# Single row maxima as two 256-key halves on both sides of a score pair, ordered by a SyncE no-op

## The chip, the cores and the metric

The kernel runs on 1 core of a Trainium2 chip. The metric is the time in device microseconds of one execution. Five engines work side by side and wait for each other by semaphores: TensorE (PE for matmuls, PEld for the loading of their weights), VectorE (DVE), ScalarE (ACT), GpSimd (POOL) and SyncE (SP), which issues most DMAs here.

## The reference

For 2048 tokens of width 512 the kernel computes two attentions with 32 heads of 16 and mixes them by a gate. Branch A is a dilated local attention over 8 positions. Branch B is full attention with one key head and one value head that all 32 query heads share. The change lies in branch B:

```python
q = (x @ wq).reshape(B, S, H, Dh).transpose(0, 2, 1, 3)
k = x @ wk
v = x @ wv
scores = einsum("bhqd,bkd->bhqk", q, k) * (Dh ** -0.5)
p = softmax(scores, axis=-1)
...
return g * a + (1 - g) * b
```

The softmax needs the maximum of each query's 2048 scores before the exponentials, since the weights of B are large.

## The kernel before, in words

Branch B is cut into 32 units (4 blocks of 512 queries, 8 groups of 4 heads). A unit has 16 steps, one for each 128 keys, so there are 512 main steps.

In step `s`, `exp_pair` (L459) forms the scores of 128 keys for 512 queries of two heads. Head `odd = 0` uses rows 0 to 63 of the array and head `odd = 1` uses rows 64 to 127, so the two matmuls run beside each other. They write a tile of two banks (`pe` in the profile), and one ScalarE exponential of 1024 columns turns it into `pexp`. A step has two such pairs, on the tiles `eb[0]` and `eb[1]`. Then `weighted` (L473) multiplies the exponentials of step `s - 1` by the values, into `po`.

The maxima of a later unit are found between these. One maximum item is 128 queries against 512 keys of one head. `fill_pair` (L339) takes two heads at once: two matmuls on the two halves of the array into the two banks of `m2` (`pm`), and one VectorE reduction. `fill_one` (L350) takes one item: one matmul on one half of the array into the single bank `m1` (`ps`), and one reduction. A third way, `fill_diff` and `fill_sum`, takes two items with the help of ScalarE; it is used in the front of the program and in the three output phases, not in main steps. A unit needs 64 items (L39 counts them in all), and its maxima enter the query tile through small DMAs that SyncE issues (`shift_d`, L449) after two GpSimd operations (L441, L442).

The order of the work is written out by the program itself while it is built. It keeps its own clocks (`clk`, `free`) with assumed durations (L45) and asks at each place whether a bank is free by then. In the main loop (from L1218) a step is: first score pair, a pair of maxima if `m2` is free, a single maximum if `m1` is free and `singles` (L841) says that one is owed, second score pair, then `weighted`. `out_phase` (L762) projects a finished block; when it comes is decided by `LEAD` (L42), the lead of the maxima in units.

Each engine executes its own list in order. A wait that stands in TensorE's list holds all that is behind it.

Of the kernel before, what the change touches and what calls it, by code (L numbers as in the profile page):

```python
# [6 lines left out]
F32 = mybir.dt.float32  # L7
F32R = mybir.dt.float32r
AF = mybir.ActivationFunctionType
# [4 lines left out]
P = 128  # L14
# [34 lines left out]
def gated_mix_kernel(ctx, tc, xt, wa, wk, wq, wo_a, wo_b, out):  # L49
# [227 lines left out]
    def place(v):  # L277
        return v if v <= NB else (v - NB - 1) % (NB - 2)
# [18 lines left out]
    half = []  # L297
    free = {"m1": 0.0, "e0": 0.0, "e1": 0.0, "po": 0.0, "d0": 24.0, "d1": 24.0}
    tasks, shifted = [], set()
    hooks, pool, done = [], 0.0, set()  # L300
# [4 lines left out]
        marks.append((ups[0] if up is None else up, end, inst.ins.name))  # L305

    def fillable():
        return bool(half) or bool(slots) and slots[0][0] < len(stacked) and stacked[slots[0][0]] <= clk["pe"]

    def unit_tile(v):  # L310
        if v not in mx:
            mx[v] = wp.tile([P, 2, 2, 4, 4], F32, name="mx", bufs=3)
            if v < 2:
                nc.scalar.activation(mx[v].rearrange("p b i t k -> p (b i t k)"), ident[:, 0:64], AF.Identity, scale=0.0, bias=mk[:, 6:7])
            else:
                nc.gpsimd.memset(mx[v], -FMAX)
            left[v] = NF // NU
        return mx[v]
# [3 lines left out]
        nc.tensor.matmul(dst, qst[place(v)][b:b + 62, pr, t * P:(t + 1) * P], kst[b:b + 62, kc * 512:(kc + 1) * 512], start=True, stop=True)  # L322

    def to_go():
        return 2 * len(slots) + len(half)
# [23 lines left out]
    def fill_one(dst=m1, key="m1"):  # L349
# [8 lines left out]
        mark(got, free[key])  # L358
        filled(v, 1)


    kd, formed, ended = [], set(), set()
    pend, todo, read_d = [[], []], [[], []], [[0.0, 0.0], [0.0, 0.0]]
# [91 lines left out]
            shifted.add(v)  # L455


    pe, pexp, exped = [], {}, {}

    def exp_pair(s, pr):  # L460
        bank, key = eb[pr], f"e{pr}"
        u, kt = divmod(s, NJ)
        for odd in range(2):
            b = 64 * odd
            nc.tensor.matmul(bank[:, odd, :], kst[b:b + 64, kt * P:(kt + 1) * P], qst[place(u)][b:b + 64, pr, :], start=True, stop=True)  # L465
        e = px.tile([P, 2, 512], F32, name="pexp", bufs=6)
        got = nc.scalar.activation(e, bank, AF.Exp, scale=SCALE)  # L467
# [368 lines left out]

    tail, first = last_rows(), [0]

    owing = [0.0]

    def singles(s):  # L841

        steps = 16 * (NU - 1) - 8 - s
        if steps <= 0 or to_go() <= 0:
            return to_go() > 0
        owing[0] += (to_go() - 1.94 * steps - 15.5 * (NJ - 4 - outs)) / steps
        owing[0] = min(owing[0], 3.0)
        if s % 16 == 0 or owing[0] < 1.0 or clk["dve"] - clk["pe"] > 1.5 and owing[0] < 2.0:
            return False
        return True  # L850

    def fill_ready(key, slack):
        if fillable() and free[key] <= clk["pe"] + slack:
            clk["pe"] = max(clk["pe"], free[key])
            if key == "m1":
                fill_one()
            elif half and (not slots or half[0][0] < slots[0][0] or slots[0][0] >= len(stacked)):
                fill_one(m2[:, 0, :], "m2")
            elif slots:
                fill_pair(m2, "m2")  # L860
            return True

    def pause(most):
        n = 0
        while n < most and slots and fillable():
            key = min(("e0", "e1", "m2"), key=lambda k: free[k])
            clk["pe"] = max(clk["pe"], free[key])
            if half:
# [355 lines left out]
    for s in range(NS + 1):  # L1224
        u, kt = divmod(s, NJ)
        if len(stacked) < NU and s >= 16 * (gone(len(stacked)) + 1):
            stack(len(stacked))
        if s < NS and kt == 0 and u not in shifted:
            while u not in shifted:
                clk["pe"] += 0.5  # L1230
                run_tasks()
                if u not in shifted and left.get(u, 1):
                    assert pause(4)
        v = min(x[0][0] for x in (half, slots, [(NU,)]) if x)
        need = left.get(v, NF // NU)
        steps = 16 * v - 6 - s
        short = need - 2.8 * max(0, steps) if v < NU else 0
        lead = (NF - to_go()) / 64 - s / 16
        order = (0, "m2", "m1", 1) if s > 1 else (1, "m2", "m1", 0) if s else ()
        k, n = outs // 4, C - (outs >= NJ - 4)  # L1240
        if outs == NJ - 4:
            if short > 0 and steps < 2:
                pause(short)
        elif due or outs < NJ and outs // NH in done and kt == 15 and NHG * (k + 1) - 1 in shaped and (lead < LEAD or s >= 16 * (NHG * (k + 2) + 1) - 1):
            if not due:
                prepare(outs, n)
                due.append(n)
            else:
                out_phase(list(range(outs, outs + 4)), due.pop(), s)
                outs += 4  # L1250
        elif short > 0 and steps < 2:
            pause(short)

        for which in order:
            if which == "m2":
                if slots or half:
# [12 lines left out]
        run_tasks()  # L1269
        run_pool()  # L1270
    assert not slots and not half and not hooks and not tasks and first[0] > 12, (len(slots), len(hooks), len(tasks), outs)


    banks = [m2[:, 0, :], eb[0][:, 0, :], eb[1][:, 0, :], m1]
# [74 lines left out]
```

## Time and profile before

| | |
|---|---|
| median of 3 runs | 1475.54 us (1474.95 to 1475.56) |
| the profiled execution | 1475.06 us, of which the span of the instructions is 1473.1 us |
| TensorE matmul busy | 1459.5 us (99%) |
| ScalarE busy | 1303.7 us (89%) |
| VectorE busy | 1141.7 us (77%) |
| GpSimd busy | 951.0 us (65%) |

The main steps run from about 285 us to 1449 us of the span, with an output phase of some 34 us at 854, 1154 and 1287 us. A row of the timeline gives the start, the duration, the engine, the line, the operation, the tiles written and read, the count of instructions merged into it, and in brackets the idle time before it with what ended it.

### The profile page before, as it was taken

To read this page: it belongs to the slowest core of one execution; us is meant where nothing else is said; L and a number is where in the kernel's file an instruction comes from. 1 tells how busy PE (TensorE), PEld (TensorE's weight loads), DVE (VectorE), ACT (ScalarE), POOL (GpSimd) and SP (SyncE) were. 2 spreads that over 40 slices of the span, in tenths; PEclk is the share of its full clock that TensorE was granted. 3 is DMA by queue.
4 is the path that set the end of the run, shared out by engine and by line. 5 is a ranking of instruction groups with operands and counts; after the bars stand their busy time and mean duration, and the time that the engine had idled before them with its cause. 6 is when DMAs were issued, how large, how long until landed. Compare 5 with 4: busy or idle time off the path is not lost.

```text
span 1473.1 us, 29510 instructions
## 1 busy us (share of the span) xinstructions
PE 1459.5 (99%) x10965; PEld 742.9 (50%) x10965; DVE 1141.7 (77%) x1837; ACT 1303.7 (89%) x1706; POOL 951.0 (65%) x1693
## 2 busy tenths in 40 slices
PE   9999999999999999999999999999999999999998
PEld 6899999733333333333333383333333743383334
DVE  6778878788888888788888878888888678778821
ACT  5888988799999999999999989999999889889994
POOL 5731997888988988888888898898851311150000
PEclk9999999999999999999999999999999999999999
DMA  6653342320211210101202111121100000000000
GB/s 227 167 168 122 97 147 64 117 71 26 71 41 49 78 49 31 67 23 67 78 13 71 42 63 48 42 71 41 42 12 12 27 16 2 1 31 1 1 2 29
DMA packets 43911, 85.66 MB, mean 58 GB/s; under 512 B 9520, under 2 KB 25960, under 8 KB 39672
## 3 DMA queue, kind: packets, MB, share of 16 engines
q1 hardware_dynamic: 36632, 44.79, 10.1%
q0 software_dynamic: 6560, 37.95, 7.8%
q8 instruction: 86, 1.41, 0.4%
q10 hardware_dynamic: 576, 1.05, 0.2%
q14 instruction: 57, 0.47, 0.1%
HBM read 57.97 MB, written 25.25 MB: 56 GB/s over the span
## 4 chain that ended last, share of the span: by engine, by line
PE 94%; ACT 2%; POOL 1%; DVE 1%; DMA 0%; issue 0%; SPq 0%; POOLq 0%; ACTq 0%
PE po L476 34%; PE pe L465 25%; PE pf L1078 10%; PE pm L322 8%; PE ps L322 5%; PE pe L776 5%; PE pd L393 3%; ACT pexp L467 1%; PE po L322 1%; PE pf L193 1%; PE pe L1279 1%; DVE mx L344 0%; DMA ad<-stage 0%; PE pm L832 0%; PE ps L1279 0%
## 5 line engine op out<-in xcount | busy, mean ns | idle before, releaser
L467 ACT ACTIVATE pexp<-pe 128x1024 f32<-128x1024 f32 x1024 | 987.6, 1023 | 70.8 <-PE pe L465 68.1
L344 DVE TENSOR_REDUCE mx<-pm 128x2 f32<-128x1024 f32 x475 | 580.2, 1221 | 176.7 <-PE pm L322 174.6
L476 PE MATMUL po<-pexp,vst 128*32 128x512 f32 x4096 | 545.5, 605 | 0.1
L465 PE MATMUL pe<-qst,kst 64*128 64x512 f32 x1984 | 518.2, 459 | 4.7 <-ACT pexp L467 2.7
L465 PEld LDWEIGHTS pe<-qst,kst 64*128 64x128 f32 x1984 | 207.8, 183 | 466.8 <-ACT pexp L467 453.8
L405 ACT ACTIVATE dd<-pd 128x512 f32<-128x512 f32 x367 | 209.1, 604 | 46.2 <-PE pd L393 32.8
L356 DVE TENSOR_REDUCE mx<-ps 128x1 f32<-128x512 f32 x333 | 226.5, 680 | 4.7 <-PE ps L322 4.7
L322 PE MATMUL ps<-kst,qst 62*128 62x512 f32 x503 | 206.5, 410 | 0.1
L322 PE MATMUL pm<-kst,qst 62*128 62x512 f32 x916 | 186.0, 397 | 0.4
L538 POOL TENSOR_TENSOR pr<-aext 128x256 f32<-128x256 f32 x256 | 182.0, 737 | 5.2 <-DMA aext<-ad 4.9
L598 POOL TENSOR_TENSOR oa<-oa,av 128x256 f32<-128x256 f32 x224 | 164.1, 732 | 15.8
L476 PEld LDWEIGHTS po<-pexp,vst 128*32 128x32 f32 x4096 | 80.6, 108 | 158.5 <-issue 150.0
L417 DVE CUSTOM_DVE_ANT_0 dd<-ps,dd 128x512 f32<-128x512 f32 x185 | 127.7, 690 | 34.8 <-PE ps L322 14.9
L417 DVE CUSTOM_DVE_ANT_0 dd<-po,dd 128x512 f32<-128x512 f32 x182 | 125.5, 690 | 30.6 <-PE po L322 13.7
L595 POOL TENSOR_TENSOR av<-aext,lg 128x256 f32<-128x256 f32 x224 | 139.3, 622 | 12.8
L393 PE MATMUL pd<-kd,qst 62*128 62x512 f32 x367 | 144.2, 402 | 2.2 <-ACT dd L405 2.2
L1078 PE MATMUL pf<-wal,xh 64*128 64x384 f32 (+1 forms) x496 | 128.8, 340 | 0.0
L1078 PE MATMUL pf<-wah,xh 64*128 64x384 f32 (+1 forms) x496 | 124.5, 339 | 0.0
L1078 PE MATMUL pf<-wah,xl 64*128 64x384 f32 (+1 forms) x496 | 123.3, 339 | 0.0
L322 PEld LDWEIGHTS ps<-kst,qst 62*128 62x128 f32 x503 | 93.0, 185 | 43.5 <-DVE mx L356 38.8
L502 POOL TENSOR_TENSOR rl<-rl,gate_t 128x16 f32<-128x16 f32 x31 | 6.8, 221 | 158.6 <-DVE rl L496 158.6
L322 PEld LDWEIGHTS pm<-kst,qst 62*128 62x128 f32 x916 | 88.4, 186 | 3.3 <-DVE mx L344 3.1
(199 smaller groups left out, 1730.7 us busy)
## 6 DMA issues: line engine op xcount, KB each, us to landing
aext<-ad POOLq DMA_DIRECT2D x32, 1056.0 KB, 5.5
ad<-stage SPq DMA_DIRECT2D x32, 384.0 KB
qst<-qd SPq DMA_DIRECT2D x62, 128.0 KB
xraw<-xt SPq DMA_DIRECT2D x16, 256.0 KB
qd<-qhi SPq DMA_DIRECT2D x16, 256.0 KB
qd<-qlo SPq DMA_DIRECT2D x16, 256.0 KB
qst<-qd SPq DMA_DIRECT2D x62, 64.0 KB
qst<-ml SPq DMA_DIRECT2D x220, 2.0 KB
```

The lines of the kernel that those rows point to most:

```text
L322: nc.tensor.matmul(dst, qst[place(v)][b:b + 62, pr, t * P:(t + 1) * P], kst[b:b + 62, kc * 512:(kc + 1) * 512], start=True, stop=True)
L344: got = nc.vector.tensor_reduce(m[:, :, pr, t, kc], dst, AX.X, ALU.max)
L356: got = nc.vector.tensor_reduce(m[:, odd, pr, t, kc:kc + 1], dst, AX.X, ALU.max)
L393: nc.tensor.matmul(dst, qst[place(v)][b:b + 62, pr, t * P:(t + 1) * P], kd[0][b:b + 62, kc // 2, :], start=True, stop=True)
L405: got = nc.scalar.activation(held[b][k], dst, AF.Relu)
L417: got = nc.vector.tensor_tensor_reduce(held[b][k], dst, held[b][k], 1.0, -FMAX, ALU.add, ALU.max, m[:, b, pr, t, kc:kc + 1])
L465: nc.tensor.matmul(bank[:, odd, :], kst[b:b + 64, kt * P:(kt + 1) * P], qst[place(u)][b:b + 64, pr, :], start=True, stop=True)
L467: got = nc.scalar.activation(e, bank, AF.Exp, scale=SCALE)
L476: nc.tensor.matmul(po[32 * i:32 * i + 32, :], vst[:, kt, :], pexp[s, i // 2][:, i % 2, :], start=(kt == 0), stop=(kt == NJ - 1))
L538: nc.gpsimd.tensor_mul(pr[:, k], q, e[:, o:o + NH, AC:2 * AC])
L598: nc.gpsimd.tensor_add(ao, ao, av)
L1078: inst = nc.tensor.matmul(home(x)[0][:, :n], l[h], r[h], start=(i == 0 and b == 0), stop=(i == 3 * C - 1 and b == 1))
```

## The change

Single maxima in main steps get another shape. `quarters` takes the last group of a unit that has both halves of the second 1024 keys left (`kc` 2 and 3) and makes four quarters of it: 256 keys, both heads. A quarter is two matmuls of 256 columns. Head 0 writes columns 0 to 255 of `m1`, head 1 writes columns 256 to 511 of the same bank, and one reduction of 2 x 256 reads them. Since both write one bank, the second must not start before the first has ended: a SyncE no-op waits for the first, and the second waits for the no-op.

`first_quarter` issues the first half. It stands right behind the first score pair if the bank counts as free there, and otherwise at the old place of single maxima, behind the pair of maxima. The second half always stands behind the second score pair of the step, whose two matmuls are then issued in reversed order (head 1 first). The tile `mx` has 6 instead of 4 columns for each row. The rule of `singles` owes up to 5 instead of 3 and asks for 0.5 or 1.5 instead of 1.0. `LEAD` goes from 1.5 to 1.75.

```diff
@@
-LEAD, M2S, M1S, MARGIN = 1.5, 0.5, 0.3, 0.12
+LEAD, M2S, M1S, MARGIN = 1.75, 0.5, 0.3, 0.12
@@ unit_tile, filled
-            mx[v] = wp.tile([P, 2, 2, 4, 4], F32, name="mx", bufs=3)
+            mx[v] = wp.tile([P, 2, 2, 4, 6], F32, name="mx", bufs=3)
...
-            nc.vector.tensor_reduce(ms, m.unsqueeze(2).to_broadcast([P, 2, 2, 8, 4]), AX.X, ALU.max)
+            nc.vector.tensor_reduce(ms, m.unsqueeze(2).to_broadcast([P, 2, 2, 8, 6]), AX.X, ALU.max)
@@
+    def quarters():
...
+            for i in range(len(slots) - 2, -1, -1):
+                if slots[i][0] == v and slots[i][3] == 2 and slots[i + 1] == slots[i][:3] + (3,):
+                    g = slots[i][:3]
+                    del slots[i:i + 2]
+                    quarter.extend(g + (kc, h) for kc in (2, 3) for h in range(2))
+                    return True
+        return False
+
+    def quarter_mm(dst, at, odd):
+        v, pr, t, kc, h = at
+        b, k = 64 * odd, kc * 512 + h * 256
+        return nc.tensor.matmul(dst, qst[place(v)][b:b + 62, pr, t * P:(t + 1) * P], kst[b:b + 62, k:k + 256], start=True, stop=True)
+
+    def quarter_max(src, at, key):
+        v, pr, t, kc, h = at
+        got = nc.vector.tensor_reduce(unit_tile(v)[:, :, pr, t, kc + 2 * h], src, AX.X, ALU.max)
...
+    def behind_it(later, sooner):
+        tc.add_manual_dep(later.ins, sooner.ins.name, mybir.DependencyInfo(mybir.DependencyClass.Sync, mybir.DependencyReason.DATA))
@@ exp_pair
-        for odd in range(2):
+        for odd in (1, 0) if beside else (0, 1):
             b = 64 * odd
             nc.tensor.matmul(bank[:, odd, :], kst[b:b + 64, kt * P:(kt + 1) * P], qst[place(u)][b:b + 64, pr, :], start=True, stop=True)
+        with_it = beside and beside.pop()
+        if with_it:
+            behind_it(quarter_mm(m1[:, 256:512], with_it[0], 1), with_it[1])
...
+        if with_it:
+            after("pe", 0, T_R / 2)
+            quarter_max(m1.rearrange("p (b k) -> p b k", b=2), with_it[0], "m1")
@@
+    def first_quarter():
+        clk["pe"] = max(clk["pe"], free["m1"])
+        relay = nc.sync.nop()
+        behind_it(relay, quarter_mm(m1[:, 0:256], quarter[0], 0))
+        beside.append((quarter.pop(0), relay))
+        owing[0] -= 1.0
@@ singles
-        owing[0] = min(owing[0], 3.0)
-        if s % 16 == 0 or owing[0] < 1.0 or clk["dve"] - clk["pe"] > 1.5 and owing[0] < 2.0:
+        owing[0] = min(owing[0], 5.0)
+        if s % 16 == 0 or owing[0] < (1.5 if free["m1"] > clk["pe"] + 0.05 else 0.5) or clk["dve"] - clk["pe"] > 1.5 and owing[0] < 2.0:
@@ main loop
             elif which == "m1":
-                if singles(s) and fill_ready("m1", M1S):
-                    owing[0] -= 1.0
+                if single and not beside and (half or quarters()) and free["m1"] <= clk["pe"] + M1S:
+                    if half:
+                        fill_ready("m1", M1S)
+                        owing[0] -= 1.0
+                    else:
+                        first_quarter()
+                        clk["pe"] += 0.1
             elif s < NS:
                 exp_pair(s, which)
+                if which == order[0]:
+                    single = singles(s)
+                    if single and not half and quarters() and free["m1"] <= clk["pe"] + 0.05:
+                        first_quarter()
```

TensorE's list shows what becomes of main steps. Before, two steps in the second quarter of the program (`pe_4182` is the first score tile, `pe_4183` the second, `pm` the pair of maxima, `ps` the single one, `po` the weighted values; qst holds the queries, kst the keys):

```order
L465 MATMUL pe_4182<-qst_76,kst 128x512 x2
L322 MATMUL pm<-kst,qst_81 128x512 x2
L322 MATMUL ps<-kst,qst_81 128x512
L465 MATMUL pe_4183<-qst_76,kst 128x512 x2
L476 MATMUL po<-pexp,vst 32x512 x4
L465 MATMUL pe_4182<-qst_76,kst 128x512 x2
L322 MATMUL pm<-kst,qst_82 128x512 x2
L465 MATMUL pe_4183<-qst_76,kst 128x512 x2
L476 MATMUL po<-pexp,vst 32x512 x4
```

The first step has a single maximum between the pair of maxima and the second score pair, the second has none. In the changed kernel, TensorE's list in the same part of the program has two steps with quarters in a row (scores are now L495, weighted values L512, quarters L379):

```order
L495 MATMUL pe_4182<-qstx,kst 128x512 x2
L379 MATMUL ps<-kst,qst_81 128x256
L322 MATMUL pm<-kst,qst_81 128x512 x2
L495 MATMUL pe_4183<-qstx,kst 128x512 x2
L379 MATMUL ps<-kst,qst_81 128x256
L512 MATMUL po<-pexp,vst 32x512 x4
L495 MATMUL pe_4182<-qstx,kst 128x512 x2
L322 MATMUL pm<-kst,qst_81 128x512 x2
L379 MATMUL ps<-kst,qst_81 128x256
L495 MATMUL pe_4183<-qstx,kst 128x512 x2
L379 MATMUL ps<-kst,qst_81 128x256
L512 MATMUL po<-pexp,vst 32x512 x4
```

The first of these steps has its first half early (ahead of the pair of maxima), the second has it late (behind the pair); the text calls them early and late steps. With the waits named, a late step on TensorE further on reads as follows (the no-op itself, which SyncE executes, is not a row of the list; its semaphore is SP_sequencer):

```order
L495 MATMUL pe_4182<-qst_80,kst 128x512 [waits Activation_49]
L495 MATMUL pe_4182<-qst_80,kst 128x512
L322 MATMUL pm<-kst,qst_77 128x512 [waits DVE_49]
L322 MATMUL pm<-kst,qst_77 128x512
L379 MATMUL ps<-kst,qst_77 128x256 [waits DVE_49]
L495 MATMUL pe_4183<-qst_80,kst 128x512 [waits Activation_49]
L495 MATMUL pe_4183<-qst_80,kst 128x512
L379 MATMUL ps<-kst,qst_77 128x256 [waits SP_sequencer_49]
L512 MATMUL po<-pexp,vst 32x512 x4
```

The first half waits for VectorE's reading of the bank, the second score pair for ScalarE's exponential of the step before, and the second half for SyncE, with the weighted values behind it in the list. Counted over the whole list, main steps with a single maximum are 315 before (and 7 of odder forms) and 4 after; main steps with quarters are 168 early and 124 late. Plain steps, with a pair of maxima and no single one, are 154 before and 183 after. The output phases stand at the same steps in both.

More of the change, by code (lines that the diff above doesn't have):

```diff
@@ L357, in fill_one @@
         free[key] = after("dve", after("pe", 0, T_R) + T_LAT, T_RED1) + 0.08
+        mark(got, free[key])
+        filled(v, 1)
+    def quarters():
+        if quarter:
+            return True
+        for v in (slots[0][0], slots[0][0] + 1) if slots and not half else ():
+            if v >= len(stacked) or stacked[v] > clk["pe"]:
+                return False
[4 more added lines that the diff above has]
+                    quarter.extend(g + (kc, h) for kc in (2, 3) for h in range(2))
+                    return True
+        return False
+    def quarter_mm(dst, at, odd):
[5 more added lines that the diff above has]
+        got = nc.vector.tensor_reduce(unit_tile(v)[:, :, pr, t, kc + 2 * h], src, AX.X, ALU.max)
+        free[key] = after("dve", clk["pe"] + T_LAT, T_RED1) + 0.08
         mark(got, free[key])
@@ L856, in fill_ready @@
                 fill_one()
+            elif not slots and not half:
+                return False
             elif half and (not slots or half[0][0] < slots[0][0] or slots[0][0] >= len(stacked)):
@@ L864, in pause @@
         n = 0
-        while n < most and slots and fillable():
+        while n < most and (slots or quarter) and fillable():
             key = min(("e0", "e1", "m2"), key=lambda k: free[k])
             clk["pe"] = max(clk["pe"], free[key])
+            if quarter and not (half and half[0][0] < quarter[0][0]):
+                dst, at = {"e0": eb[0], "e1": eb[1], "m2": m2}[key][:, :, 0:256], quarter.pop(0)
+                for odd in range(2):
+                    quarter_mm(dst[:, odd], at, odd)
+                after("pe", 0, T_R / 2)
+                quarter_max(dst, at, key)
+                n += 1
+                continue
             if half:
@@ L1270, in gated_mix_kernel @@
         run_pool()
-    assert not slots and not half and not hooks and not tasks and first[0] > 12, (len(slots), len(hooks), len(tasks), outs)
+    assert not slots and not half and not quarter and not hooks and not tasks and first[0] > 12, (len(slots), len(hooks), len(tasks), outs)
     banks = [m2[:, 0, :], eb[0][:, 0, :], eb[1][:, 0, :], m1]
```

14 lines of the change are left out of this document (7 added, 7 removed).

## The prediction

> **What bounds the kernel now.** I read the page first (busy shares, then the chain that ended last), then TensorE's two timelines over four main steps, then those of VectorE and ScalarE at the same place, and at the end the DMA queue of SyncE.
>
> ```profile
> span 1473.1 us, 29510 instructions
> PE 1459.5 (99%) x10965; PEld 742.9 (50%) x10965; DVE 1141.7 (77%) x1837; ACT 1303.7 (89%) x1706; POOL 951.0 (65%) x1693
> PE 94%; ACT 2%; POOL 1%; DVE 1%; DMA 0%; issue 0%; SPq 0%; POOLq 0%; ACTq 0%
> L467 ACT ACTIVATE pexp<-pe 128x1024 f32<-128x1024 f32 x1024 | 987.6, 1023 | 70.8 <-PE pe L465 68.1
> ```
>
> TensorE is 94% of the chain, so a main step lasts as long as its list. But ScalarE, at 89%, is close behind; it has only 70.8 us of idle time ahead of its 1024 exponentials. Whether a step that gets shorter on TensorE ends sooner is therefore read from single steps. Weight loads show where a step begins (first `pe`) and where its weighted values begin (`po`):
>
> ```profile
> 711.55 0.19 PEld L465 LDWEIGHTS pe<-qst,kst 64*128 64x128 f32 x2 [0.84 <-ACT pexp L467]
> 711.89 0.19 PEld L322 LDWEIGHTS ps<-kst,qst 62*128 62x128 f32 x1
> ...
> 713.68 0.19 PEld L465 LDWEIGHTS pe<-qst,kst 64*128 64x128 f32 x2 [0.84 <-ACT pexp L467]
> ...
> 714.21 0.18 PEld L322 LDWEIGHTS ps<-kst,qst 62*128 62x128 f32 x1 [0.22 <-DVE mx L356]
> ...
> 715.85 0.18 PEld L465 LDWEIGHTS pe<-qst,kst 64*128 64x128 f32 x2 [0.84 <-ACT pexp L467]
> ...
> 716.28 0.19 PEld L465 LDWEIGHTS pe<-qst,kst 64*128 64x128 f32 x2
> 716.75 0.16 PEld L476 LDWEIGHTS po<-pexp,vst 128*32 128x32 f32 x8 [0.28 <-issue]
> 717.75 0.18 PEld L465 LDWEIGHTS pe<-qst,kst 64*128 64x128 f32 x2 [0.84 <-ACT pexp L467]
> ...
> 718.45 0.19 PEld L465 LDWEIGHTS pe<-qst,kst 64*128 64x128 f32 x2 [0.35 <-ACT pexp L467]
> 718.88 0.16 PEld L476 LDWEIGHTS po<-pexp,vst 128*32 128x32 f32 x8 [0.24 <-issue]
> 719.87 0.19 PEld L465 LDWEIGHTS pe<-qst,kst 64*128 64x128 f32 x2 [0.84 <-ACT pexp L467]
> ```
>
> Two steps with a single maximum take 2.13 and 2.17 us (711.55 to 713.68 to 715.85), mean 2.15. The plain step behind them takes 1.90. The second plain step in a row takes 2.12: its second score pair issues 0.70 us into the step instead of 0.43, since it waits for ScalarE to finish the exponential that still reads the tile. So ScalarE allows one short step, not two; a single maximum behind a plain step fills this gap. By the program's list there are 315 steps with a single, 130 plain ones behind another kind and 24 behind a plain one: 315 x 2.15 + 130 x 1.90 + 24 x 2.12 = 975 us of the span.
>
> ```profile
> 714.03 0.40 PE L322 MATMUL pm<-kst,qst 62*128 62x512 f32 x2
> 714.27 0.43 PE L322 MATMUL ps<-kst,qst 62*128 62x512 f32 x1
> 714.28 0.65 PE L465 MATMUL pe<-qst,kst 64*128 64x512 f32 x2
> ...
> 716.19 0.40 PE L322 MATMUL pm<-kst,qst 62*128 62x512 f32 x2
> 716.43 0.40 PE L465 MATMUL pe<-qst,kst 64*128 64x512 f32 x2
> ...
> 718.45 0.50 PE L465 MATMUL pe<-qst,kst 64*128 64x512 f32 x2
> ```
>
> 512 columns stream in 0.235 to 0.24 us (714.03 to 714.27) and end in the record 0.40 after their start. At 714.27 a score matmul starts beside the single one, the other 0.22 later: the halves of the array run independently. A weight load that nothing covers adds 0.10 (718.45: 0.50 instead of 0.40).
>
> **The change part by part.** *The quarter's stream.* On either half of the array a step carries 256 columns more than a plain one.
>
> ```profile
> L1078 PE MATMUL pf<-xh,wqh 64*128 64x512 f32 x112 | 34.6, 396 | 0.0
> L1078 PE MATMUL pf<-wah,xh 64*128 64x384 f32 x368 | 92.4, 338 | 0.0
> ```
>
> 128 columns make 0.058, so 256 last 0.28 in the record and stream in 0.115. With nothing else in the way a quarter costs 0.115 where a single costs 0.25.
>
> *Early steps (168; 161 of them directly behind a plain step).* What is late next is ScalarE. The plain step took 1.90, so the second score pair cannot issue before 0.70 of this step, as in the 2.12 step above; the second half streams behind it: 2.12 + 0.115 = 2.235, which is 0.085 more than a single's 2.15. The no-op is hidden here: the first half starts at 0.35 (714.03 less 713.68) and ends at 0.63, and the second half's weights are not needed before the score pair has streamed (0.80 + 0.24 = 1.04), less 0.10, at 0.94. The other 7 early steps cost 1.90 + 0.115.
>
> *The no-op.* Three hops between engines have rows.
>
> ```profile
> 714.47 1.23 DVE L344 TENSOR_REDUCE mx<-pm 128x2 f32<-128x1024 f32 x1 [0.16 <-PE pm L322]
> 713.47 0.68 DVE L356 TENSOR_REDUCE mx<-ps 128x1 f32<-128x512 f32 x1
> 715.61 0.68 DVE L356 TENSOR_REDUCE mx<-ps 128x1 f32<-128x512 f32 x1
> 716.63 1.23 DVE L344 TENSOR_REDUCE mx<-pm 128x2 f32<-128x1024 f32 x1 [0.34 <-PE pm L322]
> 716.46 3.86 ACT L467 ACTIVATE pexp<-pe 128x1024 f32<-128x1024 f32 x4 [0.23 <-PE pe L465]
> 716.86 0.59 SPq L290 DMA_DIRECT2D qst<-qd  x1
> 693.12 5.32 SPq L453 DMA_DIRECT2D qst<-ml  x8
> ```
>
> TensorE to SyncE is 0.03 (the pair of 716.43 ends at 716.83, the DMA starts at 716.86). VectorE to a weight load is 0.06 (714.15 to 714.21). No row shows a no-op by itself. VectorE, with one wait, starts 0.04 behind the pair's end (714.43 to 714.47); ScalarE, with two, 0.10 behind (716.36 to 716.46), so one more waiting instruction costs between 0 and 0.06. I take 0.02, a third of the way, since SyncE has nothing to set up. The second half's weights then load 0.11 us after the first half's record ends.
>
> The Trainium skill ("Advanced Engine Details and Errata", Network/Comms) states 50 to 100 ns for a sequencer to read a semaphore; the rows' 0.03 and 0.06 lie at or under this. By the page two such reads would make the relay up to 0.20 instead of 0.11, an estimate that adds 11 us over the late steps.
>
> *Late steps (124).* Here nothing hides it; behind the waiting weight load stand the weighted values. 83 come directly behind an early step, where VectorE is late too: the pair there ends 0.115 later, so its reduction starts at 0.78 + 0.115 = 0.90, the quarter's 1.14 after it (714.47 to 715.61), takes 0.68 as a single's does (same 512 elements) and is seen at 2.78, which is 0.535 into the late step. Its first half then streams at 0.635 instead of 0.58 and ends at 0.915; 0.11 more for the relay, 0.10 for the weights, 0.115 to stream: 1.24. In a plain step the second score pair has streamed by 0.58 + 0.235 = 0.815. So such a step takes 1.90 + 0.425 = 2.325; the other 41, without VectorE's wait, 1.90 + 0.37 = 2.27.
>
> *Plain steps.* 164 behind another kind, 19 behind a plain one. ScalarE is not late at the former, since a late step is long.
>
> *The sum of main steps.* After: 161 x 2.235 + 7 x 2.015 + 83 x 2.325 + 41 x 2.27 + 164 x 1.90 + 19 x 2.12 + 4 x 2.15 = 1020.5 for 479 steps. Before: 975.2 for 469, and 10 of the odd forms, which become regular, at some 2.05: 995.7. The difference is +24.8.
>
> *SyncE's queue.* Each no-op also stands behind DMAs: 92 of the 292 have one to eight directly ahead, mostly two small ones of L453 at 0.66 (5.32 / 8) each. A step is longer than two or three of them, and the four loads of a new unit fall at steps where no quarter is placed. Only where GpSimd has the maxima late do they reach into the next quarter. I take 2 us; the ends are 0 and 92 x 0.66 = 61.
>
> *The rest.* 15 more matmuls stand in the second and third output phase as maxima, half an array each: 15 x 0.12 = 1.8. `LEAD` moves no output phase to another step, so 0. The wider `mx` adds columns to 32 small reductions on VectorE and memsets on GpSimd, 0: VectorE and GpSimd are idle for 23% and 35% of the span; without that cover it would be some 0.1 each, 3 us. Fewer singles on VectorE (292 for 333) gain nothing, as it bounds no step but the 83.
>
> Sum: 24.8 + 2 + 1.8 = +28.6 on the profiled execution's 1475.06 (0.5 under the median): 1504.
>
> **The rivals.** *(1) Both halves hidden and ScalarE never late*, as the written clocks assume: all quarter steps 2.015, with 0.055 more at the 83. Then 1020.5 falls by 161 x 0.22 + 83 x 0.255 + 41 x 0.255 = 67, to 1437. Against it stand the 0.35 wait at 718.45 and the record's 0.28 before any relay can begin.
>
> *(2) Faster: ScalarE is not late at the 161 early steps, the relay is as worked out.* The place is the second score pair behind a plain step, the price 0.22 each, 35 us: 1469. It decides from 0.18 on (28.6 / 161). It would need the plain steps to become longer than 1.90 or exponentials to run under their 0.965 (3.86 / 4). Nothing in the rows speaks for it but that ScalarE's other work may move.
>
> ```profile
> 705.92 0.40 PE L322 MATMUL ps<-kst,qst 62*128 62x512 f32 x1
> 705.93 0.63 PE L465 MATMUL pe<-qst,kst 64*128 64x512 f32 x2
> ...
> 708.06 0.44 PE L322 MATMUL ps<-kst,qst 62*128 62x512 f32 x1
> 708.06 0.67 PE L465 MATMUL pe<-qst,kst 64*128 64x512 f32 x2
> ```
>
> Of two singles that follow each other one is on either half, and beside both a score matmul starts at once: the partner on the free half does not wait for its place in the list. "TensorE: Matmul & The Clock Gate" of the Trainium skill (The mechanism) says that matmuls start and end strictly in program order. By that rule the pair of maxima on the free half would wait for the first half, and only 161 x 0.105 = 17 of the 35 us would be left in this rival; these rows contradict it.
>
> *(3) The wait holds only the stream, not the weights' load:* 0.10 less at 124 steps, 1492. Against it: at 714.21 the load itself waits.
>
> *(4) SyncE's queue decides:* no-ops stand behind DMAs that wait for GpSimd, +61 instead of 2: 1563. For it: batches like that at 693.12 run back to back. Against: they run ahead of TensorE there.
>
> **How the numbers follow.** A difference under 0.2% (3 us) is about what a measurement of this kernel cannot tell from none. Forecast 0.60, (1) 0.06, (2) 0.08, (3) 0.10, (4) 0.10, and 0.06 for errors of both signs near no change. Faster: 0.06 + 0.08 and 0.02 of the last, 0.16. Same: 0.03. Slower: 0.81. The no-op's ends give -2.5 and +5 us, milder forms of (4) some 25 more; (3) lies at 1492. The forecast's own range is 1490 to 1520. The range 1472 to 1535 leaves out (1), (2) and the upper half of (4), 0.19.
>
> **What would show it.** Early steps of 2.2 us with ScalarE as releaser of the second score pair; late steps of 2.27 to 2.33 with the second `ps` load waiting for SyncE, some 0.4 us behind the first half's start; the idle time ahead of `ps` loads growing to tens of us while PE's busy share falls under 99%. The prediction is wrong if early steps take 2.0, if late ones take under 2.15, or if SyncE's no-ops wait for DMAs in many steps.

## The result, and the profile after

The changed kernel takes 1496.59 us in the median (1496.13 to 1496.85), the kernel before 1475.55 us beside it (1474.95 to 1475.65). The ratio is 1.0143, with a 95% interval of 1.0126 to 1.0161: slower by 21 us, where 28.6 were forecast.

The page of the changed kernel, with the lines that answer to those of before, and the weight loads of the new matmuls:

```profile
span 1494.3 us, 30344 instructions
PE 1478.6 (99%) x11258; PEld 785.8 (53%) x11258; DVE 1137.2 (76%) x1827; ACT 1306.6 (87%) x1717; POOL 951.5 (64%) x1693
PE 92%; ACT 4%; DVE 1%; DMA 1%; issue 1%; SPq 0%; POOL 0%; ACTq 0%; POOLq 0%; DVEq 0%
L500 ACT ACTIVATE pexp<-pe 128x1024 f32<-128x1024 f32 x1024 | 986.3, 1023 | 93.3 <-PE pe L495 86.7
L379 PEld LDWEIGHTS ps<-kst,qst 62*128 62x128 f32 x560 | 103.8, 185 | 45.6 <-SPq L877 22.2
```

The span grows by 21.2 us (1473.1 to 1494.3). TensorE is as busy in share as before, VectorE and ScalarE have the same work and a smaller share of a longer span. ScalarE's idle time ahead of its exponentials grows from 70.8 to 93.3 us: it now waits for TensorE more, and still its part of the chain (the work that ended last, followed back) doubles from 2% to 4%. A new releaser is there, SyncE's no-op (`SPq L877`).

The waits of the weight loads by what released them (us in total, how often, the longest), and SyncE's own waiting:

```profile
PEld ps L379 <- SPq L877: 23.3, 123, 0.9
PEld ps L379 <- DVE mx L383: 20.1, 83, 0.3
SPq L877 <- PE ps L379: 812.5, 285, 10.0
```

By single steps, 121 of the 123 waits for SyncE are in the 124 late steps and 2 in early ones. Of the 83 waits for VectorE 78 are in the 83 late steps behind an early one, the other 5 in early steps that do not follow a plain one. The third row is no loss: at 285 of the 292 no-ops it is SyncE that waits for TensorE.

TensorE's weight loads over four steps of the changed kernel:

```profile
689.33 0.19 PEld L495 LDWEIGHTS pe<-qst,kst 64*128 64x128 f32 x2 [0.84 <-ACT pexp L500]
689.44 0.19 PEld L379 LDWEIGHTS ps<-kst,qst 62*128 62x128 f32 x1
...
690.04 0.19 PEld L495 LDWEIGHTS pe<-qst,kst 64*128 64x128 f32 x2 [0.17 <-ACT pexp L500]
690.15 0.19 PEld L379 LDWEIGHTS ps<-kst,qst 62*128 62x128 f32 x1
690.58 0.16 PEld L512 LDWEIGHTS po<-pexp,vst 128*32 128x32 f32 x8 [0.25 <-issue]
691.58 0.19 PEld L495 LDWEIGHTS pe<-qst,kst 64*128 64x128 f32 x2 [0.84 <-ACT pexp L500]
...
692.12 0.18 PEld L379 LDWEIGHTS ps<-kst,qst 62*128 62x128 f32 x1 [0.24 <-DVE mx L383]
692.12 0.29 PEld L495 LDWEIGHTS pe<-qst,kst 64*128 64x128 f32 x2
692.59 0.18 PEld L379 LDWEIGHTS ps<-kst,qst 62*128 62x128 f32 x1 [0.18 <-SPq L877]
692.90 0.16 PEld L512 LDWEIGHTS po<-pexp,vst 128*32 128x32 f32 x8
693.90 0.19 PEld L495 LDWEIGHTS pe<-qst,kst 64*128 64x128 f32 x2 [0.84 <-ACT pexp L500]
...
695.80 0.19 PEld L495 LDWEIGHTS pe<-qst,kst 64*128 64x128 f32 x2 [0.84 <-ACT pexp L500]
...
696.51 0.19 PEld L495 LDWEIGHTS pe<-qst,kst 64*128 64x128 f32 x2 [0.37 <-ACT pexp L500]
...
697.94 0.19 PEld L495 LDWEIGHTS pe<-qst,kst 64*128 64x128 f32 x2 [0.84 <-ACT pexp L500]
```

The first step (689.33, behind a plain one) is an early one and takes 2.25. Its second score pair loads 0.71 into the step and waits for ScalarE; the second half's load right behind it waits for nothing. The second (691.58) is a late step and takes 2.32: its first half waits for VectorE, its second half for SyncE, and the weighted values can begin only behind that, at 1.32 instead of the 0.90 of a plain step. Then come a plain step of 1.90 and a second one of 2.14.

The first half of the late step, from TensorE's matmuls:

```profile
692.15 0.35 PE L379 MATMUL ps<-kst,qst 62*128 62x256 f32 x1
```

It ends in the record at 692.50, and the second half's weights load at 692.59: the whole relay over SyncE takes 0.09.

The regular main steps together, worked out from the distances of the weight loads that begin them (number, mean us):

| kind of step | before | after | predicted |
|---|---|---|---|
| early, behind a plain one | | 161, 2.239 | 2.235 |
| late, behind an early one | | 83, 2.329 | 2.325 |
| late, behind a late one | | 41, 2.249 | 2.27 |
| plain, behind another kind | 130, 1.908 | 164, 1.908 | 1.90 |
| plain, behind a plain one | 24, 2.133 | 19, 2.084 | 2.12 |
| single | 315, 2.162 | 4, 2.13 | 2.15 |
| the 7 other early steps | | 7, 2.22 | 2.015 |
| sum of these | 469, 980.2 | 479, 1022.5 | 975.2 before, 1020.5 after |

### The profile page after: what moved, and what is told of

Same layout as the page of the kernel before. It is cut to its first block, busy times and chain, and to the rows that moved or that the text cites. A ratio compares the mean times of both kernels' runs of the same rounds, so it can differ in the third digit from the quotient of the medians.

```text
span 1494.3 us, 30344 instructions
## 1 busy us (share of the span) xinstructions
PE 1478.6 (99%) x11258; PEld 785.8 (53%) x11258; DVE 1137.2 (76%) x1827; ACT 1306.6 (87%) x1717; POOL 951.5 (64%) x1693
## 4 chain that ended last, share of the span: by engine, by line
PE 92%; ACT 4%; DVE 1%; DMA 1%; issue 1%; SPq 0%; POOL 0%; ACTq 0%; POOLq 0%; DVEq 0%
PE po L512 32%; PE pe L495 23%; PE pf L1131 10%; PE pm L322 8%; PE ps L379 5%; PE pe L812 5%; ACT pexp L500 4%; PE pd L419 3%; PE ps L322 2%; PE po L322 1%; PE pe L1341 1%; PE pf L193 1%; DMA ad<-stage 0%; DMA xraw<-xt 0%; DVE mx L344 0%
## 5 line engine op out<-in xcount | busy, mean ns | idle before, releaser
L500 ACT ACTIVATE pexp<-pe 128x1024 f32<-128x1024 f32 x1024 | 986.3, 1023 | 93.3 <-PE pe L495 86.7
L344 DVE TENSOR_REDUCE mx<-pm 128x2 f32<-128x1024 f32 x485 | 592.3, 1221 | 208.8 <-PE pm L322 206.3
L512 PE MATMUL po<-pexp,vst 128*32 128x512 f32 x4096 | 545.5, 605 | 0.3
L495 PE MATMUL pe<-qst,kst 64*128 64x512 f32 x1984 | 486.2, 467 | 5.1 <-ACT pexp L500 2.7
L495 PEld LDWEIGHTS pe<-qst,kst 64*128 64x128 f32 x1984 | 202.2, 183 | 467.1 <-ACT pexp L500 452.9
L431 ACT ACTIVATE dd<-pd 128x512 f32<-128x512 f32 x378 | 214.5, 604 | 42.9 <-PE pd L419 28.4
L322 PE MATMUL pm<-kst,qst 62*128 62x512 f32 x925 | 202.5, 396 | 0.1
L383 DVE TENSOR_REDUCE mx<-ps 128x2 f32<-128x512 f32 x292 | 198.7, 681 | 0.0
L379 PE MATMUL ps<-kst,qst 62*128 62x256 f32 x560 | 173.1, 309 | 0.7 <-SPq L877 0.6
L443 DVE CUSTOM_DVE_ANT_0 dd<-po,dd 128x512 f32<-128x512 f32 x188 | 129.7, 690 | 29.3 <-PE po L322 14.3
L512 PEld LDWEIGHTS po<-pexp,vst 128*32 128x32 f32 x4096 | 80.5, 108 | 127.3 <-issue 102.9
L379 PEld LDWEIGHTS ps<-kst,qst 62*128 62x128 f32 x560 | 103.8, 185 | 45.6 <-SPq L877 22.2
L322 PEld LDWEIGHTS pm<-kst,qst 62*128 62x128 f32 x925 | 114.0, 186 | 3.6 <-DVE mx L344 2.0
```

What stands on the lines that cost most here:

```text
L344: got = nc.vector.tensor_reduce(m[:, :, pr, t, kc], dst, AX.X, ALU.max)
L379: return nc.tensor.matmul(dst, qst[place(v)][b:b + 62, pr, t * P:(t + 1) * P], kst[b:b + 62, k:k + 256], start=True, stop=True)
L383: got = nc.vector.tensor_reduce(unit_tile(v)[:, :, pr, t, kc + 2 * h], src, AX.X, ALU.max)
L431: got = nc.scalar.activation(held[b][k], dst, AF.Relu)
L443: got = nc.vector.tensor_tensor_reduce(held[b][k], dst, held[b][k], 1.0, -FMAX, ALU.add, ALU.max, m[:, b, pr, t, kc:kc + 1])
L512: nc.tensor.matmul(po[32 * i:32 * i + 32, :], vst[:, kt, :], pexp[s, i // 2][:, i % 2, :], start=(kt == 0), stop=(kt == NJ - 1))
```

## The experiments

The theory was the prediction's: early steps lose because ScalarE cannot follow a second short step, late steps because they wait for the relay with nothing beside it. Against it stood that the relay is hidden and only ScalarE counts, that only the stream waits, that SyncE's queue counts, and that the halves on both sides of the array have to keep the order of the list.

**Only early halves.** At the late place stands a single maximum of 512 keys, as before.

```diff
-                if single and not beside and (half or quarters()) and free["m1"] <= clk["pe"] + M1S:
...
+                if single and not beside and (half or slots) and fill_ready("m1", M1S):
+                    owing[0] -= 1.0
```

> Quarters with an early first half are kept (97 steps, 91 behind a plain one); the place behind the pair of maxima takes old singles of 512 keys again (207 steps), so no second half waits for a no-op that nothing hides. Theory (late steps lose by the relay and by VectorE, early ones by ScalarE): late steps of 2.25 to 2.33 become singles of 2.13 to 2.19, early steps behind plain ones stay at 2.24; by the step counts the main steps fall by some 19 us, to 1476 to 1479. Rival A (only the relay costs, early steps are free): early steps 2.0, 1465. Rival B (all the loss is in early steps): 97 of 168 are left, 1488.

Measured: 1488.57 us (1487.09 to 1489.74), ratio 1.0088 [1.0072, 1.0105]. The theory's figure is missed by 10 to 12 us, and the time is the one that rival B gave. Rival B does not hold all the same: the next experiment, with no early step left, should by it have come out under 1485 and does not. The theory's price of an early step holds: the 91 behind a plain step have a median of 2.238. But their mean is 2.293, and the longest takes 4.51. This is that step, on TensorE's weight loads:

```profile
1090.75 0.19 PEld L495 LDWEIGHTS pe<-qst,kst 64*128 64x128 f32 x2 [0.84 <-ACT pexp L500]
...
1091.44 0.19 PEld L495 LDWEIGHTS pe<-qst,kst 64*128 64x128 f32 x2 [0.17 <-ACT pexp L500]
1093.35 0.18 PEld L379 LDWEIGHTS ps<-kst,qst 62*128 62x128 f32 x1 [1.72 <-SPq L877]
...
1095.26 0.29 PEld L495 LDWEIGHTS pe<-qst,kst 64*128 64x128 f32 x2 [1.43 <-issue]
```

SyncE's queue at the same time:

```profile
1089.16 9.39 SPq L479 DMA_DIRECT2D qst<-ml  x14
```

The first half has run by 1091.4, but the no-op stands behind small DMAs of 0.67 each (9.39 / 14), which have run since 1089.16, and the second half's load waits until 1093.35, 1.72 of idle time. This is the prediction's rival (4), in a few steps: four loads of the run wait for SyncE, 4.0 us together. Behind this wait TensorE is slow: its granted clock is 0.66 in the mean from 1093 to 1098, where it was 1.00 from 1090 to 1093, the weighted values take 1.66 instead of 1.06 (so the idle time of their loads is 1.43 instead of 0.84), and the next step, a single, takes 3.04. Whether the pause brought the slower clock is not shown.

What makes up the miss: the 91 early steps lie 0.055 over their median, 5.0 us together. The 52 singles that stand behind an early step take 2.230 in the mean, where singles of the kernel before take 2.162; in 47 of them the load waits for VectorE, which the theory had left out for singles; that is 3.5 us. The output phases add 1.5 (103.2 for 101.7).

**Only late halves.** The early place is taken out.

```diff
-                    if single and not half and quarters() and free["m1"] <= clk["pe"] + 0.05:
-                        first_quarter()
```

> All quarters have their first half behind the pair of maxima (290 steps, 134 of them behind another such step, 154 behind a plain one). Theory: every one takes 2.25, since the no-op is not hidden and VectorE is not late; behind a plain step the wait for ScalarE lies inside the same time. That is nearly what early and late steps take together in the changed kernel: 1496 to 1500. Rival A (only the relay costs): 166 more of them at 0.15 to 0.2, 1521 to 1530. Rival B (only early steps cost): under 1485.

Measured: 1497.09 us (1496.36 to 1499.05), ratio 1.0149 [1.0134, 1.0164]. As expected: 290 late steps of 2.261 in the mean, behind a plain step as behind a late one (2.249 in the median in both). Without early steps VectorE is hardly late, and the step is the 1.90 of a plain one with 0.35 on top, wherever it stands. In both groups the second half's weights load 0.94 into the step in the median, so the relay sets the step also where ScalarE is late. This speaks against both rivals: B wanted under 1485, A 1521 or more. So early and late halves cost nearly the same in sum, for different reasons.

**Five no-ops, four of them waited for by nothing.**

```diff
-        relay = nc.sync.nop()
-        behind_it(relay, quarter_mm(m1[:, 0:256], quarter[0], 0))
+        relays = [nc.sync.nop() for k in range(5)]
+        first_half = quarter_mm(m1[:, 0:256], quarter[0], 0)
+        for relay in relays:
+            behind_it(relay, first_half)
```

> Five no-ops instead of one stand in SyncE's list between the two halves of each quarter. In the changed kernel's trace two such instructions follow at 0.08 us, so the relay gets 0.2 to 0.3 longer. Theory: the 124 late steps take all of it (25 to 38 us), early ones what goes over the 0.18 that the score pair hides there (0 to 20 us): 1522 to 1552. Rival (late steps wait for VectorE's reading of the bank or for DMAs ahead of the no-op, not for the relay): under 1500.

Measured: 1495.34 us (1494.88 to 1496.59), ratio 1.0137 [1.0121, 1.0152]. This says nothing about the relay: the trace holds 292 no-ops, one for each quarter, and 30344 instructions as in the changed kernel; the four on which nothing depends are not there. It was the changed kernel once more, and shows how well its time repeats.

**Five no-ops that the second half waits for.**

```diff
-            behind_it(quarter_mm(m1[:, 256:512], with_it[0], 1), with_it[1])
+            second_half = quarter_mm(m1[:, 256:512], with_it[0], 1)
+            for relay in with_it[1]:
+                behind_it(second_half, relay)
```

> The changed kernel with five SyncE no-ops behind each first half instead of one, and the second half waits for all five, so that all stay in the program. Two such instructions follow each other on SyncE some 0.08 us apart, so the relay grows by 0.25 to 0.32 us. Theory (late steps wait for the relay with nothing beside it, early ones have about 0.18 us to spare): 124 late steps take the whole of it, +31 to +40 us, early ones 0.07 to 0.14 each, +12 to +24 us; 1530 to 1560, with the idle time that SyncE ends ahead of the second halves' weight loads near 70 to 90 us instead of 23. Rival (something else than the relay sets the late steps, the shown 0.18 us of waiting lies beside other work): under 1505.

Measured: 1531.26 us (1530.31 to 1534.64), ratio 1.0381 [1.0367, 1.0395], at the low end of the theory's range; the trace holds 1460 no-ops, five for each quarter. A late step, on TensorE's weight loads:

```profile
1005.01 0.18 PEld L495 LDWEIGHTS pe<-qst,kst 64*128 64x128 f32 x2 [0.84 <-ACT pexp L502]
...
1006.24 0.18 PEld L379 LDWEIGHTS ps<-kst,qst 62*128 62x128 f32 x1 [0.41 <-SPq L879]
1006.55 0.16 PEld L514 LDWEIGHTS po<-pexp,vst 128*32 128x32 f32 x8
```

Its first half, from TensorE's matmuls:

```profile
1005.58 0.34 PE L379 MATMUL ps<-kst,qst 62*128 62x256 f32 x1
```

The relay is now 1006.24 - 1005.92 = 0.32 instead of 0.09, so four more no-ops cost 0.23, or 0.057 each, less than the 0.08 of the expectation; SyncE ends 61.9 us of the idle time ahead of the second halves' loads, not 70 to 90. The late steps take all of it: behind a late one the median goes from 2.248 to 2.480 (+0.232), behind an early one from 2.314 to 2.536 (+0.222), 28.3 us over the 124 by their means. The early ones behind a plain step stay at 2.247 in the median (2.240 with one no-op): there 0.23 more is still hidden, a little more than the 0.18 that the expectation had granted. Their mean rises by 0.045, again in a few long steps. This shows that the wait is on the path in late steps and off it in early ones. No run takes the relay away where it stands; its share is shown by lengthening it.

**The second score pair in the order of the list.** Head 0 first, as everywhere else.

```diff
-        for odd in (1, 0) if beside else (0, 1):
+        for odd in range(2):
```

> The second score pair of a quarter step is issued head 0 first, as before the change. Theory: a matmul on the free half starts ahead of one that waits for the other half, so nothing changes: 1494 to 1499. Rival (matmuls start strictly in program order): in late steps head 1 waits for the first half's 0.115 on head 0's half, 124 x 0.115 = 14 us more: 1511.

Measured: 1496.61 us (1495.31 to 1497.09), ratio 1.0142 [1.0127, 1.0158], the same as the changed kernel's 1496.59. The time alone does not decide between the two, since a late step has some room there: a score pair that waited for the first half's 0.115 would have streamed by 0.93 (the prediction's 0.815 and 0.115), and the second half's weights load only at 0.94. The rows decide, on TensorE's matmuls:

```profile
692.61 0.34 PE L379 MATMUL ps<-kst,qst 62*128 62x256 f32 x1
692.61 0.58 PE L495 MATMUL pe<-qst,kst 64*128 64x512 f32 x2
```

Head 0 is first in the list now and needs the half on which the first half of the quarter streams. Yet in 119 of the 124 late steps one score matmul starts within 0.01 us of the first half and the other 0.11 or more behind it, nearly as in the changed kernel (117). The one that starts at once can only be that of the free half, head 1: it does not wait for its place in the list. The Trainium skill ("TensorE: Matmul & The Clock Gate", The mechanism) says that matmuls start and end strictly in program order; for the start of matmuls on halves of the array these rows and those of before contradict this.

**Shorter exponentials, in the changed kernel and in the one before.** This takes ScalarE away as a limit.

```diff
-        got = nc.scalar.activation(e, bank, AF.Exp, scale=SCALE)
+        got = nc.scalar.activation(e[:, :, 0:256], bank[:, :, 0:256], AF.Exp, scale=SCALE)
```

> The changed kernel with exponentials of half of the queries left out (256 columns of each score tile; the weighted values use them twice), so ScalarE is never late; TensorE's list is the same. Theory: early steps behind plain ones fall from 2.24 to 2.015 (36 us), second plain steps to 1.90 (4 us), but then VectorE is late next: its reading of the bank is seen 0.765 into the late step instead of 0.535, 0.23 more at 83 late steps (19 us). Together -20: 1475 to 1479. Rival A (early steps don't wait for ScalarE): -4 or less, 1492. Rival B (nothing is late next): -40, 1457.

> The kernel before with the same exponentials left out. Theory: only the 24 second plain steps wait for ScalarE there, 24 x 0.2: 5 us less, 1470. So the difference of the two kernels falls from 21 to some 6 us. Rival (ScalarE's share is the same in both kernels): the difference stays at 21.

Measured: the changed kernel 1474.05 us (1473.08 to 1475.87), ratio to the unchanged one before 0.9987 [0.9978, 0.9996]; the kernel before with the same edit 1462.8 us (1462.09 to 1463.24), ratio 0.9911 [0.9897, 0.9924]. The exponentials in the changed kernel's page:

```profile
L500 ACT ACTIVATE pexp<-pe 128x512 f32<-128x512 f32 x1024 | 573.0, 596 | 476.7 <-PE pe L495 468.0
```

With ScalarE at 0.596 each, the early steps behind a plain one fall from 2.240 to 2.018 in the median, nearly 1.90 + 0.115: stream alone, and the relay hidden. That is what rival (1) had assumed of these steps. The late steps behind a late one stay at 2.248, so ScalarE has no part in them. Those behind an early one get longer (2.531), since VectorE, whose work has not become shorter, is then later; this gives part of the gain back, as expected, and the time is 1 us under the expected range. In the kernel before a second plain step falls from 2.133 to 1.908 in the mean, 24 x 0.225 = 5.4 us; the other 7.9 us that it gained were not expected. The span falls by 11.9: 5.5 in the main steps, where the other kinds gain and lose little, 2.3 in the 23 last steps, most of whose maxima are replaced by last-row products, 2.7 in the three output phases with the steps that they stand in, and 1.4 in the front and the tail. What is left between the two kernels without ScalarE's limit is 11 of 21 us (6 were expected), with late steps that VectorE then makes longer.

**No two plain steps in a row, in the kernel before.** If the theory of ScalarE is right, singles set so that each plain step is followed by one gain the difference.

```diff
-        if s % 16 == 0 or owing[0] < 1.0 or clk["dve"] - clk["pe"] > 1.5 and owing[0] < 2.0:
+        least = -1.0 if bare[0] or s % 16 == 15 else 9.0 if s % 16 == 14 else 1.0
+        if s % 16 == 0 or owing[0] < least or clk["dve"] - clk["pe"] > 1.5 and owing[0] < least + 1.0:
             return False
...
-                if singles(s) and fill_ready("m1", M1S):
+                bare[0] = not (singles(s) and fill_ready("m1", M1S))
+                if not bare[0]:
                     owing[0] -= 1.0
```

> The kernel before with another rule for when a single is owed: one is asked for behind a plain step and at the last step of a unit, and not at the one ahead of it, so that 1 second plain step is left of 24, with 319 singles instead of 315. Theory: 23 x 0.22 = 5 us less, 1470 to 1471. Rival (the 0.22 returns at the step that now has the single): 1475.

Measured: 1468.78 us (1468.21 to 1470.91), ratio 0.9954 [0.9940, 0.9968]. It is faster than both kernels. The 156 plain steps take 1.911 in the mean, where the 154 of before, 24 of them behind a plain one, took 1.943. Singles take 2.160 as before (2.162), so the 0.22 does not return there, as the rival had it. The gain is 7.3 us where 5 were forecast; the plain steps explain 156 x 0.032 = 5.0 of it.

**The second half in the next step.** It moves from behind the second score pair to the head of the next step, so that the weighted values hide the relay; the first half may also stand at the end of the scores.

```diff
     for s in range(NS + 1):
         u, kt = divmod(s, NJ)
+        if beside:
+            second_half()
...
+                elif s > 1 and single and not beside and not half and quarters() and free["m1"] <= clk["pe"] + M1S:
+                    first_quarter()
```

> The changed kernel with the second half taken from behind the second score pair and put at the head of the next step, behind the weighted values (1.2 us of TensorE work), with the first half behind the first score pair or at the end of the scores, where the bank is free. By the program's list 157 steps carry a first half alone, 157 a second half alone and 150 both. Theory (the late steps' loss is the relay, the early ones' is that ScalarE cannot follow two short steps in a row): the relay is hidden, every step has 0.115 us more than the plain 1.90, which is also the mean that ScalarE allows (1.90 and 2.12 for two plain steps in a row), so steps of 2.015 to 2.05; 464 of them make 935 to 951 us where the changed kernel has 1020 for 478: some 40 to 60 us less, 1437 to 1457, under the kernel before. Rival (halves of 256 columns cost more than their stream wherever they stand): 1480 to 1500. Rival (VectorE, which then reads a quarter and a pair closely one behind the other, holds the halves at the bank): 1465 to 1480.

Measured: 1528.29 us (1525.8 to 1529.21), ratio 1.0349 [1.0335, 1.0363]. Theory and rivals are all missed. Where only the second half stands, the theory holds: 157 steps of 2.016, the relay is hidden. Steps with a first half alone behind such a step take 2.128 (149), as a second plain one does, and their second score pair waits for ScalarE in 138 of 155, so ScalarE allows less than the 2.015 expected. The loss lies in the 150 steps with both halves: 2.476. One of them, on TensorE's weight loads:

```profile
704.53 0.18 PEld L379 LDWEIGHTS ps<-kst,qst 62*128 62x128 f32 x1 [0.84 <-issue]
...
705.70 0.18 PEld L379 LDWEIGHTS ps<-kst,qst 62*128 62x128 f32 x1
706.02 0.16 PEld L512 LDWEIGHTS po<-pexp,vst 128*32 128x32 f32 x8
707.01 0.18 PEld L379 LDWEIGHTS ps<-kst,qst 62*128 62x128 f32 x1 [0.84 <-SPq L877]
```

VectorE's reading of the bank in this step:

```profile
704.96 0.69 DVE L383 TENSOR_REDUCE mx<-ps 128x2 f32<-128x512 f32 x1 [0.42 <-PE ps L379]
```

VectorE has read the bank at 705.65, 1.12 into the step, and the next quarter's first half loads at 705.70, with the weighted values behind it. In the whole run 148 such loads wait for VectorE:

```profile
PEld ps L379 <- DVE mx L383: 72.2, 148, 0.5
```

(2.476 - 2.015) x 150 = 69 us; without this the kernel would take some 1459, an estimate. It is the mechanism of the second rival, at a price that had been set far too low.

**The same with a shorter maximum of a quarter.** If VectorE holds the bank, its duration shows in these steps.

```diff
-        quarter_max(m1.rearrange("p (b k) -> p b k", b=2), at, "m1")
+        quarter_max(m1.rearrange("p (b k) -> p b k", b=2)[:, :, 0:128], at, "m1")
```

> The kernel with the second half in the next step, but VectorE's maximum of a quarter reads only 128 of the 256 keys of each head (the other 128 are left out of the maxima). A pair's maximum of 1024 elements takes 1.22 us and a quarter's of 512 takes 0.69, so one of 256 takes about 0.42. Theory (the 150 steps with both halves take 2.476 us instead of 2.015 since their first half waits until VectorE has read the bank, 1.17 us into the step, and holds the weighted values): the bank is read 0.27 earlier, so 150 x 0.27 = 40 us less, 1482 to 1494 for 1528. Rival (these steps are long since ScalarE or the no-op is late there): within 5 us of 1528.

Measured: 1487.36 us (1487.24 to 1487.99), ratio 1.0082 [1.0065, 1.0099], so 41 us less. The reduction, from the groups of this kernel's page:

```profile
L383 DVE TENSOR_REDUCE mx<-ps 128x2 f32<-128x256 f32 x312 | 132.3, 424 | 129.7 <-PE ps L379 128.2
```

And from the page of the kernel without the edit:

```profile
L383 DVE TENSOR_REDUCE mx<-ps 128x2 f32<-128x512 f32 x312 | 215.9, 692 | 145.8 <-PE ps L379 144.2
```

It takes 0.27 less, and the 150 steps fall from 2.476 to 2.213, 0.263 less; the other kinds of steps stay (2.124 and 2.021). So VectorE's reading of the bank sets them.

## Why the prediction was right, point by point

**Early steps** behind a plain one were forecast at 2.235 and take 2.239; that ScalarE sets them is shown by the shorter exponentials (2.018). The no-op is hidden there, as the prediction had it, and stays hidden with four more. The 7 other early steps were forecast at 2.015 and take 2.22: in five of them the first half waits until VectorE has read the bank, which the prediction had only for late steps.

**Late steps** behind an early one were forecast at 2.325 and take 2.329, the others at 2.27 and take 2.249. The prediction's relay was 0.11 and is 0.09. In this trace the no-op has a record of its own, as an operation of SyncE (nanoseconds, least, median and most, then the first and last start):

```profile
L877 SPq EVENT_SEMAPHORE  x292: 17/17/17, 293.0 to 1412.9; - x146
```

In the median of the 124 late steps it starts 0.031 behind the end of the first half's record, lasts 0.017, and the second half's load starts 0.043 behind it. So the hop to SyncE (0.03 forecast) and the no-op (0.02) were right, and the hop to the weight load (0.06) was too long. A further no-op costs 0.057, more than its own 0.017. The Trainium skill's 50 to 100 ns for a sequencer to read a semaphore ("Advanced Engine Details and Errata", Network/Comms) would make 0.10 to 0.20 of the two hops, if each is one such read; the rows show 0.031 and 0.043.

**The sum of main steps.** 1020.5 was forecast for the 479 regular steps of the changed kernel and 1022.5 measured; 1.5 of this difference are the 7 other early steps. The term of +24.8 is still too large by 3.1, since the side of before was taken too short: its 469 regular steps take 980.2, not 975.2. Of these 5.0 us 3.7 are singles, priced from two of them (2.15 for 2.162), and 1.4 plain steps. Its odd forms were priced well (11 take 2.03 each, 10 at 2.05 were forecast). One main step of the changed kernel has no maximum at all (1.7). So the same 480 steps take 1002.5 before and 1024.2 after, a difference of 21.7. This is the mis-sized term, on the side of before and not in the new steps.

**SyncE's queue** had 2 us. It stands within the measured steps, so nothing had to be added for it. Two early steps of the changed kernel wait for a no-op behind DMAs, the longest takes 3.14, and the kernel with early halves only has 4.0 us of such waits.

**Output phases** had +1.8: between the weighted values ahead of them and those behind they take 103.4 against 101.7, +1.7. Counted with the whole steps that they stand in it is +0.6, and the front and the tail are 1.1 shorter together, which was not forecast. So 21.7 + 0.6 - 1.1 = 21.2, the growth of the span, where 28.6 had been forecast. Four errors of one sign make the 7.4 between them: 3.1 in the main steps, 2.0 for the queue, 1.2 in the phases and 1.1 at the ends.

**The signs.** The waits stand where they were looked for: the second half's load comes 0.42 behind the first half's start in the median of the late steps, for 0.4, and the idle time ahead of all loads of quarters is 45.6 us. TensorE's busy share, which was to fall under 99%, moves from 99.1% to 98.9% only, so it hardly tells.

**The rivals.** (1), both halves hidden and ScalarE never late, and (2), ScalarE not late at early steps, needed steps of 2.015; early ones come near this (2.018) only when exponentials are cut. (3), that only the stream waits, would have given late steps of 2.15 to 2.17 behind a late one; the weights' load itself waits, with 0.18 in its row, and the steps take 2.249. (4), SyncE's queue, is real, but only 2 of the 292 no-ops start more than 0.3 behind the end of the first half.

## What to carry to other kernels

Price a step by which engine is late after it, not by the stream that it adds: with 0.115 us of columns steps were 0.34 and more over a plain one here, once because ScalarE could not follow and once because a relay stood in front of the longest block of the list. The relay between two matmuls cost time only where nothing streamed meanwhile, so put work of its length between the two, and look whether the bank is read in time for the next user; a bank that is used in each step needs its reader early in the step. Steps of uneven length lose on the engine that is nearly full, and spacing the short ones out gained 0.5% here by the order of the work alone.

## What the runs showed of the hardware that was not expected

- A whole relay from TensorE over a SyncE no-op back to a weight load takes 0.09 us from the end in the record (0.031, 0.017 and 0.043), and each further no-op 0.057.
- Of two score matmuls on different halves of the array the one on the free half starts first, also where it is second in the list (119 of 124 late steps); the reversed and the plain order in the list give 1496.59 and 1496.61 us.
- A no-op on the queue that also issues DMAs waited up to 1.7 us behind DMAs of 0.67 each, and a TensorE weight load waited with it.
- With exponentials of half the width the kernel before gained 13 us where its second plain steps account for 5.4; the rest is mostly in the last steps, in the output phases and at the ends.
